# Value products of a gated feed-forward layer: one unit of two banks with 64-row parts in two row tiles, and a new order

## The chip, the cores and the metric

The kernel runs on one core of one Trainium2 chip. The metric is the device time of one execution in microseconds (us); the kernel before has a median of 239.88 us over 3 runs (239.53 to 241.89). All data are fp32 at the interface.

## The reference, cut to what matters

First a gated linear recurrence (mLSTM) over 768 steps, for 4 batches and 8 heads of 40 columns; then, over its 320 output columns, a causal convolution of 5 taps that gates a linear layer, and a second linear layer:

```python
# x: (4, 768, 320), the recurrence's output, heads side by side
xp = np.concatenate([np.zeros((B, K - 1, D)), x], axis=1)
for k in range(K):
    gate_pre += conv_w[k][None, None, :] * xp[:, k:k + S, :]
gate = 1.0 / (1.0 + np.exp(-gate_pre))
val = x @ w_val                      # the "value products"
return gate * val @ w_out            # the "output products"
```

The weights have 320 x 320 entries.

## The kernel before

**Tiling.** The 768 steps are cut into six chunks j of 128 steps (P), each of two halves of 64 (L). The recurrence is done in its chunked form: for each chunk, batch and half there are decays (`args` on PE, `expo` on ACT), scores (`scores` on PE, `probs` on DVE), weighted keys (`keyw` on POOL), products with the values and the state (`heads` on PE, fp32), and the copy of the new state (`state` on ACT). q and k are split into fp16 parts first (`hi` on POOL or ACT, `lo` on DVE, line 387) and turned, in chunk 0 and for q of chunk 1 by PE (`turn`, `tout`), later by transposing DMAs on SP's queue (`tr`). Then `rs` (POOL) and `x` (`gate_o`, DVE, line 496) give the recurrence's output, and `x_tr` (PE) and `xc` (ACT) turn it so that its 320 columns lie on partitions: 128 and 128 in `xc`, and the last 64 in `x3`, where batches 0 and 1 lie on partitions 0 to 63 and batches 2 and 3 on 64 to 127.

**The layer behind it**, `feed_part`, works on a chunk of all four batches (chunk 5 in two halves of two batches): `conv0` (ACT) and `conv` (DVE), the sigmoid `sig` (ACT), then for each block m of 128, 128 and 64 output columns a value product `val` (PE) and the product with the gate `z` (`z_mul`, DVE, line 591), then the output products `outp` (PE, lines 599 and 601) for two batches at a time, `ob` (ACT) and the store `od` (SP).

**A value product before.** For m = 0 and 1 it has one PSUM bank of 128 partitions x 512 (four batches of 128 steps). Two products over 128 rows each take all four batches at once (line 577). The last 64 rows of the contraction lie on two halves of the partitions, so two products over 128 rows of 256 columns (line 579) take `wv3[:, i]`, a copy of the 64 weight rows in half i with zeros in the other half; the zeros are set by `fill_v` (line 814). For m = 2 (64 columns) there are six products of 256 columns that write the two halves of the partitions (line 586). In the two halves of chunk 5 (line 574) the 64 rows are taken alone, without the zeros. The output products of a pair of batches already take their last 64 rows from two halves, into two banks (line 601).

**The order.** Nothing is reordered by a scheduler: `op` collects the work, and `PLAN` gives each kind's instances a place in one list of 1146; each engine, and each DMA queue, runs its own part of that list in order. `BANKS` gives the bank of each use of PSUM. Gates of the recurrence are computed by `gates` (DVE; 0 to 11 for the first 128 steps, 12 to 22 for the rest, interleaved by `PLAN`), spread to DRAM by `spr` (DMAs issued by ACT) and gathered by `gat` (SP); `args` of chunk 0 needs them. The weights are converted by `w_v` (DVE), `w_p` (POOL) and `w_a` (ACT).

Of the kernel before, what the change touches and what calls it, by code (L numbers as in the profile page):

```python
# [31 lines left out]
    "max": (  # L32
        "30 33 46 58 65 70 75 79 86 160 230 237 241 244 258 268 280 285 304 307 310 313 328 336 361 392 436 465 "
        "468 471 475 485 614 617 627 633 636 649 655 661 663 667 679 706 759 761 771 781"
    ),
# [6 lines left out]
    ),  # L42
    "lo": (
        "110 88 107 117 153 141 158 150 308 323 303 326 312 327 298 362 425 441 404 480 398 422 432 460 545 567 "
        "570 632 517 533 550 621 680 705 748 772 697 677 714 833 823 850 849 858 836 857 870 878"
    ),
# [3 lines left out]
    "args": (  # L50
        "176 187 182 191 223 231 219 260 263 272 291 348 365 376 396 410 433 476 488 523 551 580 540 588 597 642 "
        "637 648 698 718 707 774 788 785 817 839 873 889 893 909 918 974 953 1004 1016 1032 1030 1050"
    ),
    "expo": (
        "200 203 190 210 228 247 224 265 274 278 325 358 381 399 403 439 447 482 494 528 556 582 544 592 607 644 "
        "659 683 701 743 713 779 795 791 822 842 876 897 899 913 925 979 956 1009 1019 1042 1040 1055"
    ),
    "scores": (
        "197 199 194 222 234 236 250 275 345 347 370 367 380 394 446 461 478 481 492 558 564 591 576 594 640 646 "
        "669 699 744 747 741 784 819 837 851 872 883 901 910 921 971 980 996 1011 1053 1052 1054 1067"  # L60
    ),
    "probs": (
        "209 213 201 240 245 259 277 318 352 357 374 377 387 414 452 466 483 505 508 562 572 599 586 605 647 657 "
        "673 702 753 758 751 787 827 844 855 874 886 904 919 926 983 987 1002 1018 1056 1059 1058 1070"
    ),
    "keyw": (
        "205 212 202 225 232 257 251 270 286 311 332 372 391 405 411 449 472 486 499 553 569 593 573 601 631 650 "
        "662 691 709 755 717 783 799 797 825 852 881 900 916 922 929 960 1021 1043"
    ),
    "heads": (  # L70
        "214 226 207 243 254 266 283 322 356 371 386 400 428 448 463 484 547 559 534 568 583 625 619 629 685 700 "
        "690 710 762 778 768 794 847 866 861 885 895 914 940 955 998 1013 1007 1026 1060 1069 1065 1073"
    ),
    "state": (
        "221 235 215 253 262 273 299 333 366 457 397 417 444 462 479 490 552 574 541 579 598 653 626 643 692 712 "
        "703 754 769 786 775 802 862 880 868 890 902 920 948 970 1006 1012 1066 1068"
    ),
    "nabs": (
        "249 252 294 334 395 412 493 491 565 575 639 645 719 722 793 801 879 891 961 964 1024 1031 1072 1077"
    ),  # L80
    "nrec": "264 335 429 496 581 652 724 804 894 965 1033 1081",
    "rs": (
        "276 305 355 342 431 437 510 518 585 589 665 658 728 730 807 810 911 906 967 966 1036 1035 1083 1086"
    ),
    "x": (
        "282 320 393 354 473 458 520 526 603 595 684 660 731 734 814 846 917 912 973 969 1039 1037 1087 1088"
    ),
    "x_tr": (
        "287 338 408 363 495 521 527 530 671 616 715 721 792 835 905 903 968 959 982 984 1071 1048 1089 1092"
    ),  # L90
    "xc": (
        "293 343 413 369 500 525 532 535 675 620 735 739 812 838 915 907 977 972 986 988 1074 1051 1094 1098"
    ),
    "w_d": "89 63 43 98 93 87 229 220 302 382",
    "w_v": (
        "128 146 168 177 184 192 186 188 193 195 204 216 218 227 233 242 255 269 267 271 289 329 344 368 390 401 "
        "407 419 427 438 430 442 445 454 531 557"
    ),
# [6 lines left out]
    ),  # L105
    "conv0": "515 459 506 610 681 606 757 805 766 928 930 934 994 990 992 1078 1075 1080 1109 1103 1107",
    "conv": (
# [4 lines left out]
    ),  # L112
# [7 lines left out]
    ),  # L120
    "od": (
        "634 704 727 720 773 888 843 831 892 933 944 947 1001 1003 1028 1047 1063 1064 1095 1104 1137 1140 1143 "
        "1145"
    ),
}
# [19 lines left out]
def tile_mlstm_gated_ffn(  # L145
# [13 lines left out]
    nc = tc.nc  # L159
# [703 lines left out]
```

## Time and profile before

| what | us |
|---|---|
| median of 3 runs | 239.88 |
| the profiled execution | 239.03 |
| its span, first to last instruction | 237.2 |
| PE busy | 186.5 |
| DVE busy | 189.7 |
| ACT busy | 170.0 |
| POOL busy | 118.1 |

A row of the timeline reads: start in us from the span's start, duration in us, engine, line, operation, what is written from what, shape, count, and in brackets the idle time of the engine before it with what ended it. PE is the matmul engine, PEld its weight loads, SP the queue that issues most DMAs. An fp32 product is recorded as two matmuls. The end of a matmul is modelled and lies after the start of the next, so the pace of a series is read from starts.

### The profile page before, as it was taken

The page shows a single profiled execution, that of the slowest core. Times are in us where ns is not written, and L with a number is a line of the kernel's source. Part 1 is how long each engine was busy: PE and PEld are TensorE (multiplying, and loading weights), DVE is VectorE, ACT ScalarE, POOL GpSimd, SP SyncE. Part 2 cuts the span into 40 slices and gives each one's busy share as a digit, 9 for nine tenths or more (in the row PEclk, how much of TensorE's full clock was granted, in tenths as well). Part 3 has the DMA queues.
Part 4 walks back from the last instruction along what each step waited for, and adds up shares of the span by engine and source line. Part 5 has one row for each costly group of instructions (what it writes and reads, how often), then busy time and mean ns, then how long its engine had stood idle before and what let it go on. Part 6 is the DMA issues. An engine that isn't in the chain of part 4 may idle for free.

```text
span 237.2 us, 6282 instructions
## 1 busy us (share of the span) xinstructions
PE 186.5 (79%) x2392; PEld 131.8 (56%) x2392; DVE 189.7 (80%) x409; ACT 170.0 (72%) x353; POOL 118.1 (50%) x169
## 2 busy tenths in 40 slices
PE   0003266975877589869999899999999999999993
PEld 0003263854865365556757476676766765785541
DVE  6999989789998699999989398984796874449910
ACT  6716559699989999689989898787838737247411
POOL 8969734689795566376472737822813013001000
PEclk9999999798599979999999999999999999999998
DMA  7999359999799999999999999999950101011011
GB/s 134 172 181 190 40 99 152 194 150 196 154 165 183 185 169 161 191 170 171 174 199 173 217 186 199 205 172 144 168 148 0 58 6 53 0 59 55 3 55 57
DMA packets 146599, 31.96 MB, mean 135 GB/s; under 512 B 142408, under 2 KB 145864, under 8 KB 146568
## 3 DMA queue, kind: packets, MB, share of 16 engines
q1 hardware_dynamic: 144936, 31.25, 81.4%
q10 hardware_dynamic: 1632, 0.30, 0.7%
q8 instruction: 19, 0.31, 0.6%
q14 instruction: 12, 0.10, 0.1%
HBM read 17.87 MB, written 4.23 MB: 93 GB/s over the span
## 4 chain that ended last, share of the span: by engine, by line
PE 49%; DVE 21%; ACT 12%; POOL 5%; issue 5%; DMA 5%; SPq 0%; POOLq 0%; ACTq 0%; DVEq 0%
PE pb L599 11%; PE pb L463 10%; PE pb L577 5%; PE pb L574 4%; PE pb L601 4%; DVE stk L387 3%; PE pb L503 3%; DMA tq<-stk 3%; PE pb L434 3%; PE pb L579 3%; POOL stk L383 2%; PE pb L586 2%; DVE pb L545 2%; PE pb L421 2%; ACT junk L353 2%
## 5 line engine op out<-in xcount | busy, mean ns | idle before, releaser
L463 PE MATMUL pb<-vc,pt 104*64 104x41 f32 (+1 forms) x768 | 56.5, 237 | 7.8 <-DVE pt L439 3.6
L463 PEld LDWEIGHTS pb<-vc,pt 104*64 104x64 f32 (+1 forms) x768 | 51.2, 145 | 16.9 <-ACT vc L249 5.6
L446 POOL TENSOR_TENSOR kw<-kp,dm 128x320 f32<-128x320 f32 (+1 forms) x44 | 34.1, 782 | 51.2 <-ACT dm L424 27.0
L465 PE MATMUL pb<-vc,kw 128*40 128x41 f32 (+1 forms) x704 | 44.6, 220 | 1.7 <-ACT dm L424 0.7
L439 DVE SCALAR_TENSOR_TENSOR pt<-pb,cmp,dm 128x512 f32<-128x512 f32 x48 | 35.0, 742 | 11.2 <-PE pb L434 6.4
L465 PEld LDWEIGHTS pb<-vc,kw 128*40 128x40 f32 (+1 forms) x704 | 40.0, 120 | 2.3 <-issue 0.8
L410 PE MATMUL pb<-ident,stk 128*120 128x128 f16 x96 | 12.2, 313 | 30.5 <-DVE stk L387 30.4
L387 DVE SCALAR_TENSOR_TENSOR stk<-nat,scl,stk 128x320 f16<-128x320 f32 x48 | 32.6, 701 | 0.7 <-POOL stk L383 0.6
L424 ACT ACTIVATE dm<-pb 128x512 f32<-128x512 f32 x48 | 27.6, 594 | 4.5 <-PE pb L421 4.1
L383 POOL TENSOR_SCALAR stk<-nat,scl 128x640 f16<-128x640 f32 x28 | 25.2, 906 | 9.4 <-DVE scl L359 4.1
L599 PE MATMUL pb<-wall,zt 128*128 128x320 f32 x96 | 29.2, 444 | 0.0
L410 PEld LDWEIGHTS <-stk 128*120 128x120 f16 x96 | 10.7, 213 | 31.9 <-DVE stk L387 31.8
L545 DVE SCALAR_TENSOR_TENSOR pb<-xc,cwt,pb 128x512 f32<-128x512 f32 (+1 forms) x42 | 27.3, 671 | 1.4 <-ACT pb L541 1.0
L491 POOL TENSOR_TENSOR rs<-sg,den 128x320 f32<-128x320 f32 x24 | 18.1, 770 | 19.5 <-DVE den L487 15.6
L353 ACT ACTIVATE junk<-nat 128x320 bf16<-128x320 f32 x48 | 22.5, 468 | 6.0 <-DMA nat<-in_q_dram 3.4
L249 ACT COPY vc<-pb 40x328 f32<-40x328 f32 x44 | 18.9, 432 | 9.4 <-PE pb L465 7.6
L249 POOL COPY kp<-nat 64x640 f32<-64x640 f32 x24 | 22.5, 944 | 1.3
L249 ACT COPY ob<-pb 128x320 f32<-128x320 f32 x24 | 9.6, 426 | 17.3 <-PE pb L601 13.6
L434 PEld LDWEIGHTS <-tk 120*128 120x128 f16 x384 | 15.5, 100 | 11.1 <-issue 8.3
L434 PE MATMUL pb<-tq,tk 120*128 120x64 f16 x384 | 18.0, 196 | 4.5 <-ACT dm L424 2.6
L599 PEld LDWEIGHTS pb<-wall,zt 128*128 128x128 f32 x96 | 17.3, 190 | 7.6 <-issue 1.3
L577 PE MATMUL pb<-xc,wall 128*128 128x512 f32 x40 | 19.4, 607 | 0.5 <-ACT xc L249 0.5
(107 smaller groups left out, 350.0 us busy)
## 6 DMA issues: line engine op xcount, KB each, us to landing
sg<-in_o_gate_dram SPq DMA_DIRECT2D x6, 640.0 KB
vc<-in_v_dram SPq DMA_DIRECT2D x12, 320.0 KB
out_dram<-ob SPq DMA_DIRECT2D x24, 160.0 KB
nat<-in_q_dram SPq DMA_DIRECT2D x10, 320.0 KB
nat<-in_k_dram SPq DMA_DIRECT2D x10, 320.0 KB
nat<-in_q_dram SPq DMA_DIRECT2D x4, 160.0 KB
nat<-in_k_dram SPq DMA_DIRECT2D x4, 160.0 KB
raw<-in_moe_w_val_dram SPq DMA_DIRECT2D x2, 320.0 KB
```

The costliest lines, as they stand in the source:

```text
L249: (e.copy if e is nc.scalar else e.tensor_copy)(out, in_)
L383: nc.gpsimd.tensor_scalar(o, v, f, 1.0, op0=ALU.mult, op1=ALU.mult)
L387: nc.vector.scalar_tensor_tensor(t[:, :, lo : lo + D], part(j, x, i), scl[j % 2][:, x, i : i + 1], t[:, :, 0:D], op0=ALU.mult, op1=ALU.sub ...
L424: nc.scalar.activation(dm_[g % NDM], psd[g], AF.Exp)
L434: nc.tensor.matmul(pss[g][:, h], tk[h], tq[:, h], start=True, stop=True)
L439: nc.vector.scalar_tensor_tensor(pt_[g % NPT], pss[g], cmp_[j % 2][:, p, b : b + 1], dm_[g % NDM], op0=ALU.mult, op1=ALU.mult)
L446: eng("keyw", "P").tensor_mul(kw_[g % NKW][0:n], kp[0:n, p, b * H : (b + 1) * H], dm_[g % NDM][0:n, :, L - 1 : L].to_broadcast([n, H, D]),)
L463: nc.tensor.matmul(ph[u][p * L : (p + 1) * L, h], pt_[g % NPT][0:n, h], mv, start=True, stop=True)
L465: nc.tensor.matmul(pc[g][n0 : n0 + D, h], kw_[g % NKW][0:n, h], mv, start=True, stop=True)
L545: nc.vector.scalar_tensor_tensor(of(gt, c, b0, b1) if t == 4 else o, x, w, o, op0=ALU.mult, op1=ALU.add)
L577: nc.tensor.matmul(pf, wv[:, c, ms], x[:, c, :, 4:], start=(c == 0), stop=False)
L599: nc.tensor.matmul(t, zz[0][:, c, b], wo[:, c], start=(c == 0), stop=False)
```

## The change

For chunks 0 to 4, the value products of m = 0 and m = 1 (the weight columns, that is output rows 0 to 255 of the turned result) become one unit. It has two banks, one for each pair of batches, and each bank holds both blocks m side by side. Eight products of 256 columns take the first 256 rows; then four products of 64 rows take the last rows of each pair from its own half of the partitions, without zeros. `z_mul` now reads one bank, that is both blocks of one pair of batches. m = 2 and chunk 5 are computed as before. The zeros of `wv3` are only set for the 64 columns of m = 2. `PLAN` and `BANKS` are new throughout, with 1141 places; of their lines those that are spoken of are shown.

```diff
--- before.py
+++ after.py
@@ -16,123 +16,123 @@
...
 PLAN = {
-    "ld_g": "3 0",
-    "ld_q0": "13 21 26 32 35 24 28 47",
...
-    "gates": "27 42 34 37 55 62 66 77 91 95 103 105 29 49 44 57 68 84 99 119 123 129 134",
...
+    "ld_g": "35 32",
+    "ld_q0": "15 0 26 39 6 17 75 56",
...
+    "gates": "59 137 80 105 120 141 156 167 168 169 171 173 83 109 138 117 124 150 174 176 178 180 182",
...
-    "w_d": "89 63 43 98 93 87 229 220 302 382",
...
+    "w_d": "71 64 61 23 67 97 234 243 302 423",
...
-    "val": "415 507 498 674 725 733 821 853 840 962 946 975 1038 1044 1034 1096 1123 1112 1129 1118 1105",
-    "z": "578 590 584 736 740 746 863 867 865 978 976 981 1045 1049 1041 1127 1130 1122 1134 1132 1131",
-    "outp": "600 654 749 800 875 924 985 1017 1057 1076 1133 1135 1138 1141",
...
+    "val": "562 505 713 689 853 820 947 964 1014 1026 1090 1104 1099 1117 1122 1111",
+    "z": "588 583 580 729 731 727 872 870 862 969 967 973 1028 1031 1032 1123 1121 1120 1127 1129 1128",
+    "outp": "599 652 742 789 883 925 978 1002 1038 1071 1126 1130 1133 1136",
...
 BANKS = {
...
-    "val": "073310251234640712230",
-    "outp": "311751541632526116626547",
...
+    "val": "270507314471263371406",
+    "outp": "403206323674017663512173",
...
@@ -562,33 +562,44 @@
 
     vt, pot = {}, {}
 
-    def val(n, j, m, b0, b1):
+    def val(n, j, ms, b0, b1):
         x, y = xc[j % 2], x3[j % 2]
-        ms = slice(m * P, min(DM, m * P + P))
-        pf = vt[j, m, b0] = bank("val", n, b1 - b0 if m < 2 else B2, P)
+        cs = [slice(m * P, min(DM, m * P + P)) for m in ms]
+        ts = [bank("val", n + i, 2 * B2 if ms[0] < 2 and b1 - b0 == B else B2, P) for i in range(len(ms))]
+        vt[j, ms[0], b0] = ts
         if b1 - b0 < B:
             r = half(b0)
-            o = pf if m < 2 else pf[r]
-            mm = [(wv[:, c, ms], x[:, c, b0:b1, 4:]) for c in range(2)] + [(wv3[r, b0 // B2, ms], y[r, :, 4:])]
+            o = ts[0] if ms[0] < 2 else ts[0][r]
+            mm = [(wv[:, c, cs[0]], x[:, c, b0:b1, 4:]) for c in range(2)] + [(wv3[r, b0 // B2, cs[0]], y[r, :, 4:])]
             for i, (w, s) in enumerate(mm):
                 nc.tensor.matmul(o, w, s, start=(i == 0), stop=(i == len(mm) - 1))
-        elif m < 2:
-            for c in range(2):
-                nc.tensor.matmul(pf, wv[:, c, ms], x[:, c, :, 4:], start=(c == 0), stop=False)
-            for i in range(2):
-                nc.tensor.matmul(
-                    pf[:, i * B2 : (i + 1) * B2], wv3[:, i, ms], y[:, :, 4:], start=False, stop=(i == 1)
-                )
+        elif len(ms) == 2:
+            for m in range(2):
+                for c in range(2):
+                    for i, t in enumerate(ts):
+                        o = t[:, m * B2 : (m + 1) * B2]
+                        nc.tensor.matmul(
+                            o, wv[:, c, cs[m]], x[:, c, i * B2 : (i + 1) * B2, 4:], start=(m == 0 and c == 0), stop=False
+                        )
+            for m in range(2):
+                for i, t in enumerate(ts):
+                    r = half(i * B2)
+                    o = t[:, m * B2 : (m + 1) * B2]
+                    nc.tensor.matmul(o, wv3[r, i, cs[m]], y[r, :, 4:], start=False, stop=(m == 1))
         else:
             for c in range(3):
                 for i in range(2):
-                    w, s = (wv[:, c, ms], x[:, c, i * B2 : (i + 1) * B2, 4:]) if c < 2 else (wv3[:, i, ms], y[:, :, 4:])
-                    nc.tensor.matmul(pf[i * L : i * L + L], w, s, start=(c == 0), stop=(c == 2))
-
-    def z_mul(j, m, b0, b1):
-        s = vt[j, m, b0]
-        s = s[half(b0)] if m == 2 and b1 - b0 < B else s
-        nc.vector.tensor_mul(of(zz, m, b0, b1), s, of(gt, m, b0, b1))
+                    w, s = (wv[:, c], x[:, c, i * B2 : (i + 1) * B2, 4:]) if c < 2 else (wv3[:, i], y[:, :, 4:])
+                    nc.tensor.matmul(ts[0][i * L : i * L + L], w[:, cs[0]], s, start=(c == 0), stop=(c == 2))
+
+    def z_mul(j, m, i, b0, b1):
+        s = vt[j, m, b0][i]
+        if b1 - b0 == B and m == 0:
+            bs = slice(i * B2, (i + 1) * B2)
+            nc.vector.tensor_mul(zz[0][:, :, bs], s.rearrange("p (m b) t -> p m b t", m=2), gt[0][:, :, bs])
+        else:
+            s = s[half(b0)] if m == 2 and b1 - b0 < B else s
+            nc.vector.tensor_mul(of(zz, m, b0, b1), s, of(gt, m, b0, b1))
 
     def outp(j, bs):
         n = j * B + (2 * bs[0] if len(bs) > 1 else bs[0])
@@ -728,9 +739,10 @@
             for t in range(5):
                 op("conv" if t else "conv0", conv, n, j, c, t, b0, b1)
         op("sig", sigmoid, j, b0, b1)
-        for m in range(3):
-            op("val", val, seen.get("val", -1) + 1, j, m, b0, b1)
-            op("z", z_mul, j, m, b0, b1)
+        for ms in ((0, 1), (2,)) if b1 - b0 == B else ((0,), (1,), (2,)):
+            op("val", val, 3 * j + ms[0] + 3 * (b0 // B2), j, ms, b0, b1)
+            for i in range(len(ms)):
+                op("z", z_mul, j, ms[0], i, b0, b1)
         for bs in [(b, b + B2) for b in range(B2)] if b1 - b0 == B else [(b,) for b in range(b0, b1)]:
             op("outp", outp, j, bs)
             for b in bs:
@@ -811,7 +823,7 @@
             for t, r0 in ((wv3, 0), (wo3, L)):
                 for i in range(2):
                     if t is wv3:
-                        op("w_p", fill_v, "w_p", "P", t[L - i * L : P - i * L, i], 0.0)
+                        op("w_p", fill_v, "w_p", "P", t[L - i * L : P - i * L, i, 2 * P :], 0.0)
                     op("w_a", copy, "w_a", "A", t[i * L : i * L + L, i], w3[r0 : r0 + L])
             for c in range(2):
                 weights(wo[:, c], [w_out[c * P : (c + 1) * P]], 3 + c)
```

In the new list the unit of a chunk stands before its m = 2 product in chunks 3 and 4 and after it in chunks 0 to 2.

## Rows read from the trace of the kernel before

**Rows 1.** The page, part 1: busy us, share of the span, instructions.
```profile
PE 186.5 (79%) x2392; PEld 131.8 (56%) x2392; DVE 189.7 (80%) x409; ACT 170.0 (72%) x353; POOL 118.1 (50%) x169
```

**Rows 2.** Windows: stretch, length; busy (count) of PE, PEld, DVE, ACT, POOL; clock, DMA.
```profile
0.00:41.00 41.00, 11.12 (x101) 8.75 (x102) 36.80 (x96) 24.17 (x41) 28.98 (x49) 1.00 0.86 139
41.00:89.00 48.00, 36.46 (x664) 29.75 (x661) 42.40 (x86) 43.09 (x102) 34.91 (x44) 0.86 1.07 174
89.00:136.00 47.00, 41.64 (x605) 28.96 (x605) 41.52 (x89) 40.80 (x89) 26.87 (x36) 1.00 1.27 181
136.00:233.60 97.60, 97.26 (x1031) 64.31 (x1029) 68.95 (x143) 61.53 (x124) 27.34 (x42) 1.00 0.51 95
```

**Rows 3.** The chain of waits, its end: start us, us, what.
```profile
232.77 0.75 PE pb L601 x2
...
233.59 0.43 ACT ob L249
```

**Rows 4.** Timeline of PE, 134 to 139.5 us.
```profile
134.58 1.08 PE L586 MATMUL pb<-xc,wall 128*64 128x256 f32 x8 [1.05 <-DVE x L496]
...
136.74 2.40 PE L599 MATMUL pb<-wall,zt 128*128 128x320 f32 x8
```

**Rows 5.** The chain of waits, 120 to 146 us.
```profile
124.62 6.52 DMA tq<-stk
```

**Rows 6.** Timeline of DVE, 133.5 to 136.8 us.
```profile
134.03 0.49 DVE L496 TENSOR_TENSOR x<-pb,rs 128x320 f32<-128x320 f32 x1 [3.41 <-POOL rs L491]
...
135.18 1.62 DVE L591 TENSOR_TENSOR zt<-pb,sg 128x512 f32<-128x512 f32 x3
```

**Rows 7.** Timeline of PE, 195.8 to 202.7 us: value products of chunk 4.
```profile
197.31 1.98 PE L577 MATMUL pb<-xc,wall 128*128 128x512 f32 x4
199.13 1.03 PE L579 MATMUL pb<-x,wall 128*128 128x256 f32 x4
199.99 1.88 PE L577 MATMUL pb<-xc,wall 128*128 128x512 f32 x4
201.71 1.03 PE L579 MATMUL pb<-x,wall 128*128 128x256 f32 x4
202.57 0.38 PE L503 MATMUL pb<-ident,x 128*128 128x128 f32 x2
```

**Rows 8.** Timeline of PE, 191.3 to 194.3 us: output products of two batches.
```profile
193.53 0.81 PE L601 MATMUL pb<-wall,zt 64*128 64x320 f32 x4
194.27 0.25 PE L463 MATMUL pb<-vc,pt 104*64 104x41 f32 x1
```

**Rows 9.** Timeline of PE, 220.3 to 223.8 us: value products of chunk 5.
```profile
220.35 1.13 PE L574 MATMUL pb<-xc,wall 128*128 128x256 f32 x4
221.41 0.70 PE L574 MATMUL pb<-x,wall 64*128 64x256 f32 x2
222.04 1.13 PE L574 MATMUL pb<-xc,wall 128*128 128x256 f32 x4
```

**Rows 10.** Groups by shape: busy us, mean ns | idle before, releaser.
```profile
L387 DVE SCALAR_TENSOR_TENSOR stk<-nat,scl,stk 128x320 f16<-128x320 f32 x48 | 32.6, 701 | 0.7 <-POOL stk L383 0.6
...
L591 DVE TENSOR_TENSOR zt<-pb,sg 128x512 f32<-128x512 f32 x10 | 6.7, 686 | 3.6 <-PE pb L579 3.6
```

**Rows 11.** Timeline of SP's queue, 0 to 22 us.
```profile
1.20 0.41 SPq L832 DMA_DIRECT2D sg<-in_f_gate_dram  x1
1.65 0.43 SPq L336 DMA_DIRECT2D nat<-in_q_dram  x1
...
8.68 0.58 SPq L336 DMA_DIRECT2D nat<-in_q_dram  x1
```

**Rows 12.** Timelines of DVE, 0 to 42 us: first scan, last gate step, `probs`.
```profile
3.58 0.41 DVE L293 TENSOR_TENSOR_SCAN zt<-sg,ig 32x128 f32<-32x128 f32 x1 [1.30 <-DMA sg<-in_f_gate_dram]
...
21.32 0.69 DVE L305 TENSOR_TENSOR gsp<-ob,gsp 64x128 bf16<-64x128 f32 x1
...
40.99 0.74 DVE L439 SCALAR_TENSOR_TENSOR pt<-pb,cmp,dm 128x512 f32<-128x512 f32 x1
```

More of the change, by code (lines that the diff above doesn't have):

```diff
@@ L56 @@
-        "659 683 701 743 713 779 795 791 822 842 876 897 899 913 925 979 956 1009 1019 1042 1040 1055"
+        "229 247 244 240 277 288 272 293 316 327 340 361 358 378 392 403 417 502 515 491 591 578 596 614 641 647 "
+        "670 679 695 744 716 749 767 821 777 818 838 897 877 915 926 980 907 982 1036 1027 1039 1059"
     ),
     "scores": (
-        "197 199 194 222 234 236 250 275 345 347 370 367 380 394 446 461 478 481 492 558 564 591 576 594 640 646 "
-        "669 699 744 747 741 784 819 837 851 872 883 901 910 921 971 980 996 1011 1053 1052 1054 1067"
+        "241 226 246 258 284 289 291 307 324 332 359 356 396 384 401 419 485 495 501 531 584 587 594 634 642 677 "
@@ L61 @@
+        "681 686 708 760 753 758 807 817 812 831 880 909 878 914 972 992 945 994 1033 1046 1048 1062"
     ),
     "probs": (
-        "209 213 201 240 245 259 277 318 352 357 374 377 387 414 452 466 483 505 508 562 572 599 586 605 647 657 "
-        "673 702 753 758 751 787 827 844 855 874 886 904 919 926 983 987 1002 1018 1056 1059 1058 1070"
+        "245 254 249 264 295 298 303 310 337 341 363 373 400 440 413 426 490 506 520 535 597 592 601 637 649 685 "
+        "690 693 715 769 756 764 813 830 822 837 884 911 890 920 981 997 962 1017 1040 1049 1054 1065"
@@ L72 @@
-        "690 710 762 778 768 794 847 866 861 885 895 914 940 955 998 1013 1007 1026 1060 1069 1065 1073"
+        "250 267 260 275 300 317 326 338 344 362 375 391 406 451 422 439 526 537 543 557 615 628 621 645 668 696 "
+        "702 728 732 775 765 782 828 840 845 869 904 918 896 938 988 1009 998 1030 1050 1064 1060 1066"
     ),
     "state": (
-        "221 235 215 253 262 273 299 333 366 457 397 417 444 462 479 490 552 574 541 579 598 653 626 643 692 712 "
-        "703 754 769 786 775 802 862 880 868 890 902 920 948 970 1006 1012 1066 1068"
+        "263 280 270 283 312 323 333 352 355 438 386 399 415 465 436 482 533 546 554 564 624 636 630 654 684 703 "
@@ L77 @@
+        "710 733 739 803 774 800 832 871 859 874 913 928 902 946 999 1004 1056 1063"
     ),
     "nabs": (
-        "249 252 294 334 395 412 493 491 565 575 639 645 719 722 793 801 879 891 961 964 1024 1031 1072 1077"
+        "278 287 335 346 370 427 489 497 567 563 643 653 705 735 784 793 863 881 959 957 1023 1034 1067 1069"
     ),
-    "nrec": "264 335 429 496 581 652 724 804 894 965 1033 1081",
+    "nrec": "290 347 437 500 568 656 736 794 882 960 1037 1070",
     "rs": (
-        "276 305 355 342 431 437 510 518 585 589 665 658 728 730 807 810 911 906 967 966 1036 1035 1083 1086"
+        "299 304 357 365 446 442 504 509 573 571 660 662 747 746 802 799 885 888 963 965 1044 1043 1073 1075"
@@ L84 @@
     ),
     "x": (
-        "282 320 393 354 473 458 520 526 603 595 684 660 731 734 814 846 917 912 973 969 1039 1037 1087 1088"
+        "308 360 367 377 460 448 512 514 579 575 663 671 773 748 847 849 891 917 977 979 1057 1045 1079 1080"
     ),
     "x_tr": (
-        "287 338 408 363 495 521 527 530 671 616 715 721 792 835 905 903 968 959 982 984 1071 1048 1089 1092"
+        "313 372 388 382 468 463 522 534 595 589 755 683 810 836 875 912 968 970 983 985 1068 1058 1083 1086"
     ),
     "xc": (
-        "293 343 413 369 500 525 532 535 675 620 735 739 812 838 915 907 977 972 986 988 1074 1051 1094 1098"
+        "348 380 394 389 484 470 528 539 605 600 761 687 815 841 887 919 971 975 989 991 1072 1061 1091 1095"
@@ L93 @@
     ),
[L94 removed]
+    "w_d": "71 64 61 23 67 97 234 243 302 423",
     "w_v": (
[L96 to L98 removed]
[3 rows of a table removed]
+        "88 113 140 142 149 170 154 186 192 204 224 227 233 235 238 239 259 268 271 279 315 321 379 393 407 416 "
+        "434 445 464 473 467 471 477 479 494 503"
+    ),
[3 rows of a table added]
     "tr": (
[2 rows of a table removed]
[2 rows of a table added]
     ),
[L106 removed]
+    "conv0": "450 447 519 612 609 603 805 780 770 930 936 922 995 1001 1018 1074 1081 1076 1097 1109 1107",
@@ L107 @@
     "conv": (
[4 rows of a table removed]
-    ),
[4 rows of a table removed]
[4 rows of a table added]
+    ),
[4 rows of a table added]
     "ob": (
[2 rows of a table removed]
[2 rows of a table added]
     ),
     "od": (
-        "634 704 727 720 773 888 843 831 892 933 944 947 1001 1003 1028 1047 1063 1064 1095 1104 1137 1140 1143 "
-        "1145"
+        "620 743 707 709 762 850 848 844 898 903 944 942 987 990 1015 1013 1052 1053 1088 1092 1132 1135 1138 "
+        "1140"
     ),
@@ L126 @@
 BANKS = {
-    "turn": "201374652700",
-    "args": "013456165235714473316523713617154535223300255357",
-    "scores": "562421362335334446426665740463237430556467135033",
-    "ph": "074165124125022674107247",
-    "pc": "23352155227733552542007447647733036065443010205",
-    "x_tr": "261154424465732057130204",
-    "conv": "675650004756046513564",
-    "val": "073310251234640712230",
-    "outp": "311751541632526116626547",
+    "turn": "035214670217",
+    "args": "456253054116722220154136320117150322715637044021",
+    "scores": "432504700614456444555014006335324055110067647044",
+    "ph": "623501366516421627255123",
+    "pc": "44375644173345241133224470663034305631416020700",
+    "x_tr": "766401332772034403237672",
+    "conv": "724753757036037640552",
+    "val": "270507314471263371406",
+    "outp": "403206323674017663512173",
 }
```

18 lines of the change are left out of this document (8 added, 10 removed), and 60 rows, old and new, of the table PLAN.

## The prediction

> **What bounds the kernel now.** I read the page first, for the share of each engine: no engine is busy for more than 80% of the span, DVE 189.7 us and PE 186.5 us [rows 1]. Such shares are means over stages, so I cut the span where the picture changes. Up to 136 us PE works for 11.12 + 36.46 + 41.64 = 89.2 us and is idle for 46.8; from 136 to 233.6 us it works for 97.26 us of 97.60 [rows 2]. In that second part nothing but PE sets the pace: the chain of waits ends in output products on PE, back to back, and one copy [rows 3]. So the end of PE is its work plus its idle time ahead: 186.5 + 47.1 = 233.6 us. A change moves the end by what it takes out of PE's work, and by what it adds to or takes from those 47 us.
>
> What makes the 47 us is mostly DVE: it is busy 36.80 of the first 41.00 us, 42.40 of the next 48.00 and 41.52 of the next 47.00 [rows 2]. It is the bound up to about 120 us, with ACT close behind it from 41 to 89 us (43.09 of 48.00). The last idle of PE before it fills up comes at 134.58 us, where a value product waits 1.05 us for its bank, whose last reader is `gate_o` (L496) on DVE; PE is at the first output products of chunk 1 at 136.74 us [rows 4], right behind the z products of DVE at 135.18 us [rows 6]. That x and these z products hang on a transposing DMA of 6.52 us, which held a slot of `stk` [rows 5].
>
> **The unit, step by step.** An fp32 product is two passes in the records (eight records of L577 for the four instructions of chunk 4 [rows 7]). Four passes of 512 columns run from 197.31 to 199.13 us, the first of them after another shape; in the next product they run from 199.99 to 201.71, 1.72 us, 0.43 each. Four passes of 256 columns take 199.13 to 199.99, 0.86 us, 0.215 each [rows 7]. One product of 128 rows is thus 1.72 + 0.86 = 2.58 us, or 2.68 where it begins after another shape; both together 5.26 as in chunk 4, or 5.36 where other work stands between them, as in chunks 0 to 3 of before.
>
> The new unit has the same columns for the first two thirds of the contraction, cut in 256s: 2 m x 2 c x 2 banks x 2 passes = 16 passes x 0.215 = 3.44 us (eight passes of 512 cost 8 x 0.43 = 3.44 too). For the last 64 rows before spends 8 passes of 256 columns, half of whose weights are zeros: 1.72 us. The new unit gives each pair of batches only its own 64 rows. Do two such passes run side by side? L601 is the nearest row: four records of 320 columns with 64 rows, two halves into two banks, take 193.53 to 194.27, 0.74 us; one after the other they would take 4 x 0.267 = 1.07, in pairs 2 x 0.267 = 0.53 and two changes of shape. So they pair [rows 8]. The change of shape I price at L574: four full passes and the step to 64 rows are 220.35 to 221.41, 1.06 us = 4 x 0.215 + 0.20, that is 0.10 at the entry and 0.10 at the step; the two 64-row passes 221.41 to 222.04, 0.63 = 2 x 0.215 + 0.20 [rows 9]. For the new unit: 0.10 entry + 3.44 + 0.10 + four paired passes 0.86 + 0.20 = 4.70 us. Against 5.30 (mean of 5.26 and 5.36) a unit saves 0.60, or 0.70 where no change of shape stands at its start; five units, 3.0 to 3.5 us, say 3.2. Bounds: if each second batch of 64-row passes did not pair, 8 x 0.215 stands for 4 x 0.215 and the unit is 5.56, 1.0 to 1.5 us lost over five; if no change of shape cost anything, 4.30 and 5 us gained. I take the paired value, for L601 has the same row halves and the same two banks.
>
> A rule that speaks against the change: the Trainium skill, TensorEngine Tiling (Array Packing), Key Properties, says that changing the tiling mode, not just the tile, drains the engine. If that meant waiting until the last full pass is out, whose record lasts 0.38 us (1.03 less three steps of 0.215) [rows 7], a step would cost 0.17 instead of 0.10 us. Two steps in each of five units would then make the saving 0.7 us smaller, 2.5 us. The trace has the step at 0.10, so I stay with that.
>
> **What else the change moves.** The z products stay ten of 512 elements, 686 ns each [rows 10], each now reading one bank with both blocks of rows instead of one block with all batches. They wait for the whole unit instead of one product; the output products needed all of them anyway, so that costs nothing as long as the order puts other PE work between (4 to 8 PE steps do in the new list). The two memsets of zeros shrink from 320 to 64 columns on POOL, in a stretch where POOL has room: nothing.
>
> **The new order** is the larger unknown. At the start it asks for the gates as the 7th and 8th load instead of the 1st and 2nd. Before, the second of them goes out at 1.20 us and the first scan runs at 3.58; q and k loads go out at 1.65 to 8.68 us [rows 11, 12]. Eight issues at 0.5 to 0.8 us put the gates' landing near 8 us, and the last half of chunk 0's q (now the 16th) near 14 to 17. The new order gives DVE 6.6 us of constants ahead of the scan, so only 1 to 2 us of that is idle; later DVE stands at the scales of the last batch and at the first tap conversion, some 2 to 5 us. The gates are ready near 34 us instead of 21.32 + 0.69 [rows 12], and the first `probs` of batch 0 come near 50 instead of 40.99 us. This is mostly work drawn forward: summed over the lists with the records' durations, DVE has 36.3 us ahead of those `probs` in the old order (its busy time to 41 us, 96 instructions, is 36.80 [rows 2]) and 45.3 in the new one, seven `lo` steps of chunk 1 (701 ns each [rows 10]) and five weight conversions being most of the difference. Ahead of the first `probs` of chunk 2 both orders have the same, 79.0 and 79.3 us (79.2 is DVE's busy time up to 89 us [rows 2]); the sigmoid of chunk 0 has 2.5 us more ACT work ahead, that of chunk 1 0.5 us less. So by chunk 2 the new kernel is level if DVE loses no more than the 10 us it loses now up to 89 us. Against it stand 2 to 4 us more of idling at the start; for it, that there is less room for small waits later, and that the z products of chunk 1 no longer stand behind an x of chunk 3, where DVE now idles 3.41 us behind that DMA [rows 5, 6]. I take these as equal: PE's idle time stays 47 us, give or take 4.
>
> **Sum.** 3.2 us off 239.03 us (span 237.2 and 1.8 around it) is 235.8 us for the profiled execution. The median of the runs shown is 239.88, 0.85 more, so 236.7 us.
>
> **Rivals.** (1) The start costs more than it gives: the late gates and the q load behind the taps hold DVE for more than 6 us over before, and the work drawn forward doesn't pay that back by 136 us. From 3.2 us of extra PE idle the gain is gone; 6 to 9 us give 242.5 to 246. For it: DVE has little idle to catch up with [rows 2]. Against: the equal sums at chunk 2. Chance 0.13. (2) The front runs ahead: the DMA wait [rows 5] goes and PE fills up 2 to 4 us earlier: 231.5 to 234.5 us. Chance 0.17. (3) The front is 2 to 3 us late and eats most of the saving: 238 to 241 us. Chance 0.17. (4) The 64-row passes don't pair: 5.56 us a unit, 240 to 241.5. L601 speaks against it. Chance 0.05. (5) The unit waits for banks: it needs two free at once where a product needed one, and waits such as the 1.05 us at 134.58 [rows 4] come once a unit, 3 us in all: 239 to 240. In the Trainium skill the same page, Gotcha 1: PSUM Pressure, says that row tiles must write to different banks and so raise the pressure on PSUM; the two banks of the unit are that. Against it: from 136 us on PE has 0.3 us of idle in all [rows 2], so the old banks come free early, and the new list leaves 5 or more steps between release and unit in most chunks. Chance 0.06.
>
> **Numbers.** The forecast, 234.8 to 238 us, has 0.42. A measurement of this kernel can tell about 1% (2.4 us) from no change. Faster by over 1% (under 237.5): 0.37 of the forecast and rival 2, 0.54. Slower by over 1% (over 242.3): rival 1 and a little of 3 and 4, 0.17. The rest, 0.29, is within 1%. The range 231.5 to 242 leaves out most of rival 1 and the far side of rival 2.
>
> **What would show it.** The unit: from its first pass to the next product 4.6 to 4.7 us, 64-row records starting in pairs; 5.5 us means rival 4. PE idle up to its full stretch near 47 us, and nothing after; a wait before the first pass of a unit, ended by a reader of its bank, is rival 5. First `probs` near 50 us and those of chunk 2 at 87 to 92; later than 94 us is rival 1. What would make me wrong most easily is a load or DMA at the start that lands later than its bytes suggest, since DVE works strictly in order and everything of chunk 0 is behind it.

## The result, and the profile after

The changed kernel takes 237.11 us (median of 4 runs, 236.31 to 237.54), the kernel before 239.99 on the same chip (4 runs): ratio 0.988, 95% interval 0.9836 to 0.9924. That is 1.2% faster, 2.9 us. The forecast was 236.7 us. Here and below, medians are over all runs of a kernel, while ratios, and the differences in us worked out from them, leave out the few runs that fell into a slower state of the chip.

The profiled execution took 236.31 us, with a span of 234.5. Its page, part 1, answers to [rows 1]:

```profile
PE 183.6 (78%) x2432; PEld 135.4 (58%) x2432; DVE 190.0 (81%) x409; ACT 169.4 (72%) x353; POOL 113.4 (48%) x169
```

PE has 2.9 us less work; the other engines but POOL are where they were. The windows, with the columns of [rows 2]:

```profile
0.00:41.00 41.00, 7.44 (x64) 6.63 (x64) 38.03 (x98) 22.91 (x47) 25.49 (x47) 0.84 0.99 153
41.00:89.00 48.00, 37.85 (x718) 30.61 (x719) 41.55 (x84) 46.32 (x104) 32.78 (x43) 0.85 1.12 170
89.00:136.00 47.00, 44.31 (x641) 33.47 (x641) 42.84 (x90) 40.05 (x80) 28.13 (x39) 0.93 1.20 181
136.00:231.00 95.00, 93.95 (x1011) 64.67 (x1009) 67.60 (x139) 59.68 (x125) 27.05 (x42) 1.00 0.54 93
```

Until 136 us PE works for 89.60 us, before for 89.22: it starts later and makes it up. It ends at 230.90 us, so its idle time is 230.90 - 183.55 = 47.3 us, before 47.0. Work fell by 2.9, idle rose by 0.3, the end came 2.6 us earlier. The end is still output products (now L610 and L612) back to back, in the chain of waits, as [rows 3]:

```profile
228.89 1.27 PE pb L610 x4
230.16 0.75 PE pb L612 x2
230.98 0.42 ACT ob L249
```

The unit of chunk 3 in PE's timeline, to be held against [rows 7], and the z products of chunk 1 with the first output product behind them, against [rows 4, 6]:

```profile
134.59 0.70 PE L610 MATMUL pb<-wall,zt 128*128 128x320 f32 x2
...
173.51 3.70 PE L581 MATMUL pb<-xc,wall 128*128 128x256 f32 x16
177.14 1.14 PE L588 MATMUL pb<-x,wall 64*128 64x256 f32 x8
178.21 1.08 PE L593 MATMUL pb<-xc,wall 128*64 128x256 f32 x8
```

```profile
132.21 0.42 DVE L602 TENSOR_TENSOR zt<-pb,sg 128x256 f32<-128x256 f32 x1 [0.89 <-ACT sg L558]
132.55 1.28 DVE L599 TENSOR_TENSOR zt<-pb,sg 128x512 f32<-128x512 f32 x2
```

The unit takes 173.51 to 178.21, 4.70 us. Sixteen passes take 3.63 us to the first 64-row record, then eight records of 64 rows 1.07: four pairs of 0.216, which is 0.86, and 0.21 for the change of shape in and behind them. The groups by shape (busy us, mean ns, then idle before) show that no unit waited for a bank in this execution, and that z products cost what they cost before:

```profile
L581 PE MATMUL pb<-xc,wall 128*128 128x256 f32 x80 | 18.5, 384 | 0.0
L588 PE MATMUL pb<-x,wall 64*128 64x256 f32 x40 | 5.7, 402 | 0.0
```

```profile
L599 DVE TENSOR_TENSOR zt<-pb,sg 128x512 f32<-128x512 f32 x10 | 6.4, 682 | 1.4 <-ACT sg L558 1.3
```

### The profile page after: what moved, and what is told of

Same layout as the page of the kernel before. It is cut to its first block, busy times and chain, and to the rows that moved or that the text cites. A ratio compares the mean times of both kernels' runs of the same rounds, so it can differ in the third digit from the quotient of the medians.

```text
span 234.5 us, 6368 instructions
## 1 busy us (share of the span) xinstructions
PE 183.6 (78%) x2432; PEld 135.4 (58%) x2432; DVE 190.0 (81%) x409; ACT 169.4 (72%) x353; POOL 113.4 (48%) x169
## 4 chain that ended last, share of the span: by engine, by line
PE 41%; ACT 17%; DVE 13%; DMA 12%; SPq 8%; issue 5%; POOL 1%; ACTq 1%; POOLq 0%; DVEq 0%
PE pb L463 12%; PE pb L610 9%; DVE pb L545 5%; DMA tk<-stk 5%; PE pb L581 5%; SPq L336 5%; PE pb L612 3%; DMA sg<-in_o_gate_dram 3%; ACT junk L353 3%; PE pb L421 3%; PE pb L434 3%; DMA nat<-in_q_dram 2%; ACT sg L558 2%; SPq L844 2%; PE pb L503 2%
## 5 line engine op out<-in xcount | busy, mean ns | idle before, releaser
L463 PE MATMUL pb<-vc,pt 128*64 128x41 f32 (+1 forms) x768 | 54.5, 236 | 6.2 <-ACT vc L249 4.8
L463 PEld LDWEIGHTS pb<-vc,pt 128*64 128x64 f32 (+1 forms) x768 | 49.9, 143 | 13.7 <-ACT vc L249 6.2
L465 PE MATMUL pb<-vc,kw 128*40 128x41 f32 (+1 forms) x704 | 44.1, 218 | 0.6 <-ACT x L249 0.2
L439 DVE SCALAR_TENSOR_TENSOR pt<-pb,cmp,dm 128x512 f32<-128x512 f32 x48 | 34.4, 736 | 11.0 <-PE pb L434 8.6
L383 POOL TENSOR_SCALAR stk<-nat,scl 128x640 f16<-128x640 f32 x28 | 26.0, 938 | 21.4 <-DMA vc<-in_v_dram 10.3
L387 DVE SCALAR_TENSOR_TENSOR stk<-nat,scl,stk 128x320 f16<-128x320 f32 x48 | 32.1, 688 | 4.9 <-POOL stk L383 2.5
L545 DVE SCALAR_TENSOR_TENSOR pb<-xc,cwt,pb 128x512 f32<-128x512 f32 (+1 forms) x42 | 27.4, 673 | 3.6 <-ACT pb L541 3.1
L610 PE MATMUL pb<-wall,zt 128*128 128x320 f32 x96 | 29.1, 442 | 0.1
L381 ACT ACTIVATE stk<-nat,scl 128x640 f16<-128x640 f32 x20 | 16.0, 823 | 9.9 <-DMA gda<-gsp 5.3
L610 PEld LDWEIGHTS pb<-wall,zt 128*128 128x128 f32 x96 | 17.3, 190 | 7.8 <-issue 1.3
L434 PE MATMUL pb<-tq,tk 120*128 120x64 f16 x384 | 18.6, 196 | 4.0 <-ACT vc L249 2.3
L421 PE MATMUL pb<-ra,la 120*128 120x512 bf16 x48 | 18.1, 404 | 1.1 <-DVE sg L545 0.9
```

The source lines that it names most:

```text
L383: nc.gpsimd.tensor_scalar(o, v, f, 1.0, op0=ALU.mult, op1=ALU.mult)
L387: nc.vector.scalar_tensor_tensor(t[:, :, lo : lo + D], part(j, x, i), scl[j % 2][:, x, i : i + 1], t[:, :, 0:D], op0=ALU.mult, op1=ALU.sub ...
L434: nc.tensor.matmul(pss[g][:, h], tk[h], tq[:, h], start=True, stop=True)
L439: nc.vector.scalar_tensor_tensor(pt_[g % NPT], pss[g], cmp_[j % 2][:, p, b : b + 1], dm_[g % NDM], op0=ALU.mult, op1=ALU.mult)
L463: nc.tensor.matmul(ph[u][p * L : (p + 1) * L, h], pt_[g % NPT][0:n, h], mv, start=True, stop=True)
L465: nc.tensor.matmul(pc[g][n0 : n0 + D, h], kw_[g % NKW][0:n, h], mv, start=True, stop=True)
```

## The experiments: unit and order apart

My theory: the end is PE's work and a front that VectorE and ScalarE set; the unit saves 3.3 us of work in any order, and the new order by itself is neutral. First rival: the new order made the gain.

**The new order without the unit.** In `val`, the loops of the unit give way to the two old products; `z_mul` takes one block again, and the fill of zeros is that of before (cut at the three dots):

```
-            for m in range(2):
+            for m, t in enumerate(ts):
                 for c in range(2):
-                    for i, t in enumerate(ts):
...
+                    nc.tensor.matmul(t, wv[:, c, cs[m]], x[:, c, :, 4:], start=(c == 0), stop=False)
+                for i in range(2):
+                    nc.tensor.matmul(
+                        t[:, i * B2 : (i + 1) * B2], wv3[:, i, cs[m]], y[:, :, 4:], start=False, stop=(i == 1)
+                    )
...
+            nc.vector.tensor_mul(of(zz, i, b0, b1), s, of(gt, i, b0, b1))
```

> The order of work and the banks of the changed kernel, but the two products of 128 output rows of chunks 0 to 4 done as before: one batch range of 512 columns after the other, the 64-row parts over 128 rows filled up with zeros, and one bank for each product. Theory (the unit's shorter work is the whole gain): two products take 5.3 to 5.4 us where the unit takes 4.7, so five times 0.67 us come back, 237.1 + 3.3 = 240.4 us, 239.6 to 241.2, and PE's busy time is 186.5 to 187. Rival (the new order made the gain): 237.1 to 238 us. Rival (the new order costs, and the unit brought more than the difference of the two kernels shows): above 241.2 us.

Measured: 238.58 us, ratio to the kernel before 0.9963 (0.9923 to 1.0002). The changed kernel, run again later beside the kernel before:

> The changed kernel itself, for the comparisons with the other runs on one chip. If its gain over the kernel before is 2.9 us as first measured: 237.1 us; if part of that was the chip: 237.5 to 238.2 us.

It took 237.26 us, ratio 0.9888 (0.9844 to 0.9932). So the new order alone is worth 0.9 us, between nothing and 1.8, and the unit in it some 1.9 (0.9963 less 0.9884, the mean of the two ratios, of 239.7 us), give or take 1.4, where I had 3.3. The profiled executions show where the rest may have gone. PE's work differs by 3.0 us (186.54 and 183.55), its end by 2.2 (233.10 and 230.90), its idle time by 0.8 the other way. PE's timeline around 146 us, with the old products in the new order:

```profile
145.87 0.81 PE L606 MATMUL pb<-wall,zt 64*128 64x320 f32 x4
146.61 0.41 PE L434 MATMUL pb<-tq,tk 120*128 120x64 f16 x8
...
148.00 0.39 PE L434 MATMUL pb<-tq,tk 120*128 120x64 f16 x8
```

and in the changed kernel, in the first of its two profiled executions (236.31 us):

```profile
144.68 0.81 PE L612 MATMUL pb<-wall,zt 64*128 64x320 f32 x4
145.90 0.39 PE L434 MATMUL pb<-tq,tk 120*128 120x64 f16 x8 [0.41 <-ACT vc L249]
...
147.91 0.39 PE L434 MATMUL pb<-tq,tk 120*128 120x64 f16 x8
```

and in the second, of the run above (238.10 us):

```profile
146.08 0.81 PE L612 MATMUL pb<-wall,zt 64*128 64x320 f32 x4
146.82 0.41 PE L434 MATMUL pb<-tq,tk 120*128 120x64 f16 x8
...
148.21 0.39 PE L434 MATMUL pb<-tq,tk 120*128 120x64 f16 x8
```

In the first, PE is 1.19 us ahead of the old products at these output products and 0.09 ahead at 148 us: it waited for ScalarE's copies. Of the 1.19, though, 0.47 were there ahead of the first unit. In the second, PE is 0.21 us behind at both places: it loses nothing here, but it waits 0.49 and 0.97 us at 159 and 162 us. The same kernel thus ends at 230.90 us in one execution and at 232.68 in the other, 2.2 and 0.4 us ahead of the one execution with the old products. What holds in both, and in the profiled executions of the two later runs that keep these units (other pass order, gates first), is this: the unit of chunk 3 saves 0.64 us and that of chunk 4 0.55, and PE loses nothing behind them. What the units of chunks 0, 1 and 2 save, 0.1 to 0.65 us each at once, is kept or waited away, another way in each execution.

**The unit without row tiles.** The 64-row parts go over 128 rows, half zeros, and the fill of zeros is that of before:

```
-                    nc.tensor.matmul(o, wv3[r, i, cs[m]], y[r, :, 4:], start=False, stop=(m == 1))
+                    nc.tensor.matmul(o, wv3[:, i, cs[m]], y[:, :, 4:], start=False, stop=(m == 1))
```

> The changed kernel, with the same unit of two banks and the same order of its full products, but the 64-row parts over all 128 rows of a zero-filled weight, so that no two passes lie in different row tiles. Theory (the row tiles make the gain): eight passes of 216 ns in place of four pairs, without the two changes of shape, 24 x 216 + 83 = 5.27 us for the unit against 4.69, so five times 0.58: 237.1 + 2.9 = 240.0 us, 239.2 to 240.8. Rival (the two banks and the alternation of the full passes make the gain): unit near 4.7 us, 237.1 us, 236.5 to 237.8.

Measured: 239.32 us, ratio 0.9989 (0.995 to 1.0027). The unit of chunk 3 in its timeline of PE:

```profile
176.53 3.70 PE L581 MATMUL pb<-xc,wall 128*128 128x256 f32 x16
180.07 1.89 PE L587 MATMUL pb<-x,wall 128*128 128x256 f32 x8
181.89 1.08 PE L592 MATMUL pb<-xc,wall 128*64 128x256 f32 x8
```

5.36 us against 4.70, and 5.26 to 5.36 for the two old products: the two banks give nothing, the row tiles all of the unit's saving.

**The 64-row passes in another order.**

```
-            for m in range(2):
-                for i, t in enumerate(ts):
+            for i, t in enumerate(ts):
+                for m in range(2):
```

> The changed kernel, with the 64-row passes of a unit in another order: the two products of one pair of batches (one row tile) first, then the two of the other, so that only the middle pass has a neighbour in the other row tile. Theory (a pass runs beside its neighbour only, so the alternation of the row tiles makes the pairs): the four records of one tile follow each other at 216 ns, then the other four, the unit takes 4.7 + 3 x 0.216 = 5.3 to 5.5 us, and the time is 237.1 + 3 to 4 = 240 to 241 us. Rival (the engine takes a later pass of the other tile ahead, or 64-row passes overlap whatever their order): unit 4.7 us, 236.5 to 237.8 us.

Measured: 237.81 us, ratio 0.9914 (0.9877 to 0.9952). My theory fell. The unit of chunk 3:

```profile
175.28 3.70 PE L581 MATMUL pb<-xc,wall 128*128 128x256 f32 x16
178.91 1.14 PE L588 MATMUL pb<-x,wall 64*128 64x256 f32 x8
179.98 0.87 PE L593 MATMUL pb<-xc,wall 128*64 128x256 f32 x6
```

4.70 us again: eight records in 1.07 us are four pairs, though the program has four passes of one row tile ahead of the four of the other. The records do not name the row tile. But two 64-row passes of a single row tile, in the kernel before, follow one another: 0.63 us [rows 9], where a pair would take 0.42. So the passes of the second row tile run beside those of the first, without alternating in the program.

This run also bears on what a unit is worth. Over the three measurements with units of 4.7 us (0.988, 0.9888, 0.9914) and the two with 5.3 us in the same order (0.9963, 0.9989) the means differ by 0.0082, or 2.0 us, give or take 0.9.

**The unit in the old order.** The code of the unit with the order and banks of before, each unit at the later place of its two products (chunk 0: slot 507 in place of 415 and 507). Against the plan of the kernel before:

```
-    "val": "415 507 498 674 725 733 821 853 840 962 946 975 1038 1044 1034 ...",
+    "val": "507 498 725 733 853 840 962 975 1044 1034 ...",
```

> The unit of the changed kernel in the order and the banks of the kernel before; the unit stands where the later of its two products stood. Theory (the unit's shorter work is the whole gain, and the idle time at the front is the same in both orders): 240.0 - 3.3 = 236.7 us, 236.2 to 237.5. Rival (the new order made the gain, or is needed for it: the unit's first product waits longer, its z products crowd): 239 to 240.5 us, with new waits of PE beside the units.

Measured: 241.88 us, ratio 1.009 (1.0052 to 1.0128): 2.2 us slower than before, not 3.3 faster. Nor did the rival foresee a loss of this size. My next theory was the late place: the first product of chunk 0 stood in a stretch where PE idles. One run moves that product alone, in the kernel before:

```
-    "val": "415 507 498 ...",
+    "val": "506 507 498 ...",
```

> The kernel before, with nothing changed but the place of one product: the product of output rows 0 to 127 of chunk 0 goes from slot 415, where PE otherwise idles near 77 us, to slot 506, beside the second product. Theory (the unit in the old order lost by this place: 2.7 us of work leave the idle stretch, PE idles 5 us there and then runs at half the clock for some us): 242 to 245 us against 239.7, with 5 us of idle time near 77 us and slow passes behind it. Rival (the place is nothing, since the front is set by VectorE and ScalarE, and the unit itself is what costs in the old order): 239.5 to 240.5 us.

Measured: 240.17 us, ratio 1.0038 (1.0012 to 1.0064), 0.9 us (0.3 to 1.5): it may be a part of the 2.2, but not the whole. Another puts the units of chunks 1 to 4 early and leaves chunk 0 alone (again against the plan of before):

```
+    "val": "415 507 498 688 733 829 853 957 975 1038 1034 ...",
...
-    "val": "073310251234640712230",
+    "val": "073310215234640712230",
```

> The order of the kernel before, with the unit in chunks 1 to 4 at the place of the earlier of its two products, or as close to it as two banks are free (slots 688, 829, 957 and 1038), and chunk 0 with the two old products at their old places (no two banks are free there early). Theory (the unit saves its shorter work in any order, and the unit in the old order lost by its late places: the first product of chunk 0 no longer ran in the 5 us in which PE idles near 77 us): four times 0.67 us less than the kernel before, 239.7 - 2.7 = 237.0 us, 236.4 to 238.2, and PE's idle time near 47 us again. Rival (the unit does not go with the old order at all, by its banks or its z products): 239.5 to 242 us, with waits of PE at the units.

In it I had overlooked two argument products of chunk 3 (slots 698 and 707) in a bank of chunk 1's unit, so a part of that chunk's values is overwritten and the products wait on one another; its 245.18 us tell nothing of the question. With free banks:

```
-    "val": "415 507 498 688 733 ...",
+    "val": "415 507 498 702 733 ...",
-    "args": "013456165235714473316523713617154535223300255357",
+    "args": "013456165235714473316523713617654535223300255357",
```

> As the run before with units at early places in the old order, but with two banks that are free: the unit of chunk 1 at slot 702, and one argument product of chunk 3 in another bank. Chunk 0 keeps its two old products. Theory (the unit saves 0.67 us in each of four chunks in any order, as long as no product loses its cover): 239.7 - 2.7 = 237.0 us, 236.2 to 238.2. Rival (the old order does not go with units, whatever their place): 239.5 to 242 us.

Measured: 245.29 us, ratio 1.0234 (1.0187 to 1.0282), 5.6 us slower: this theory fell too. Its trace shows where. Up to 123 us PE runs the instructions of the kernel before in their order, 2.5 us later in this execution. The lag is 5.9 us behind the products of chunk 1, 7.9 behind those of chunk 2, 7.4 at the end. PE's timeline (in this kernel L587 and L594 are the unit, L599 the product of 64 output rows), then VectorE's:

```profile
125.34 0.31 PE L463 MATMUL pb<-vc,pt 128*64 128x41 f32 x2 [1.28 <-ACT junk L353]
...
127.13 0.25 PE L463 MATMUL pb<-vc,pt 128*64 128x41 f32 x1 [0.66 <-DVE x L496]
...
129.79 3.72 PE L587 MATMUL pb<-xc,wall 128*128 128x256 f32 x16
133.44 1.14 PE L594 MATMUL pb<-x,wall 64*128 64x256 f32 x8
...
138.95 1.69 PE L599 MATMUL pb<-xc,wall 128*64 128x256 f32 x8 [1.96 <-DVE x L496]
```

```profile
136.00 0.17 DVE L475 TENSOR_SCALAR den<-pb 128x8 int32<-128x8 int32 x1 [3.66 <-PE pb L463]
...
138.41 0.49 DVE L496 TENSOR_TENSOR x<-pb,rs 128x320 f32<-128x320 f32 x1 [1.18 <-POOL rs L491]
```

Three things add up. Where the first product filled a wait, PE now waits (1.28 and 0.66 us). The block of 4.7 us stands ahead of a step of heads (L463) for which VectorE waits 3.66 us and then, for POOL, another 1.18; then PE waits 1.96 us for VectorE. In the kernel before VectorE waited 3.41 us in this place, for POOL alone [rows 6], and PE 1.05 [rows 4], so 1.4 and 0.9 us of this are new. And behind that wait PE is slow, by 0.5 us (a lag of 5.4, then of 5.9); windows with the granted clock third from the end:

```profile
136.98:138.95 1.97, 0.01 (x2) 0.00 (x1) 0.73 (x2) 1.97 (x1) 1.97 (x3) 1.00 1.07 201
138.95:142.69 3.74, 3.74 (x36) 2.37 (x37) 2.85 (x6) 3.65 (x9) 2.91 (x7) 0.55 1.01 167
142.69:145.80 3.11, 3.11 (x18) 1.76 (x15) 3.08 (x5) 1.61 (x5) 0.48 (x1) 1.00 0.46 93
```

The last of these runs keeps the units to chunks 3 and 4:

```
+    "val": "415 507 498 674 725 733 821 853 840 957 975 1038 1034 ...",
```

> The kernel before with the unit in chunks 3 and 4 alone, at slots 957 and 1038, where PE is never idle; chunks 0 to 2 keep their two products and their places. Theory (the unit saves its shorter work where PE is full, and what the old order lost with units it lost in chunks 0 to 2, where VectorE and ScalarE set the pace and a block of 4.7 us in PE's queue makes them wait): 239.4 - 1.1 = 238.3 us, 237.5 to 239.0. Rival (a unit costs in the old order wherever it stands): 240 us and more.

Measured: 239.63 us, ratio 1.0008 (0.9972 to 1.0045): no loss, and not the 1.1 us either. In its trace the lag behind the kernel before is 1.09 us ahead of chunk 3's products and 1.09 behind them: the 0.55 us are lost again in the two places where the two products had stood, 0.30 in the first, with a wait of 0.22 us that they had covered, and 0.25 in the second, with one of 0.09. Chunk 4's unit gains 0.55. So in the old order the unit costs in chunks 1 and 2, where VectorE and ScalarE set the pace, and saves little behind. How the loss with late units (2.2 us) divides between the three was not taken apart further.

**The start.**

```
-    "ld_g": "35 32",
+    "ld_g": "-1 -2",
```

> The changed kernel with its two gate loads first in SP's queue, as near as the kernel before had them. Theory (the late start is made up before 60 us since VectorE and ScalarE fill the time with other work, so the start does not set the end): 0 to 1 us less than the changed kernel. Rival (the late first probs, 49.2 against 41.0 us, cost time that a start as before would give back): 2 to 4 us less.

Measured: 236.75 us, ratio 0.9877 (0.9833 to 0.9921) beside 0.9888 for the changed kernel: 0.3 us less, give or take 1.5: no difference that can be told. The late gates cost nothing that these runs show.

**The tail.** Six half products of the last chunk make way for one unit and one product of 64 output rows, both at slots behind the last xc; the z products stay per half:

```
-    "val": "... 1014 1026 1090 1104 1099 1117 1122 1111",
+    "val": "... 1014 1026 1096 1109",
-    "z": "... 1031 1032 1123 1121 1120 1127 1129 1128",
+    "z": "... 1031 1032 1115 1115 1127 1128",
```

> The changed kernel with the value products of the last chunk in one unit too (both pairs of batches, 4.7 us, the full passes of the first pair of batches ahead) and one product of 64 output rows (1.45 us), where the changed kernel takes six half products of 1.6 to 1.7 us (9.9 us); its z products per half of the batches. Theory that PE alone sets the end: 3.7 us less than the changed kernel. Theory that the front of the last chunk is set by VectorE and ScalarE (taps of the second half to 223.1 us, its sigmoid, its z products to 225.2 us, then two output products of 2.03 us): the end of PE goes from 230.9 to 229.3 us, 1.6 us less than the changed kernel, 1.0 to 2.0. Rival (the z products and the taps get into each other's way): no gain, or up to 1 us more.

Measured: 242.46 us, ratio 1.0073 (1.0032 to 1.0115), 1.7 us more than the kernel before and 4.4 us more than the changed kernel by the ratios. PE's timeline and windows (in this kernel L588 is the product of 64 output rows, L606 the output products):

```profile
219.22 0.60 PE L588 MATMUL pb<-x,wall 128*64 128x256 f32 x4
223.62 2.16 PE L606 MATMUL pb<-wall,zt 128*128 128x320 f32 x4 [3.80 <-DVE sg L545]
...
227.07 2.50 PE L606 MATMUL pb<-wall,zt 128*128 128x320 f32 x4
```

```profile
219.80:223.60 3.80, 0.02 (x2) 0.00 (x0) 3.58 (x9) 0.63 (x2) 0.00 (x0) 1.00 0.00 0
223.60:227.10 3.50, 3.48 (x7) 1.48 (x7) 1.59 (x3) 1.04 (x2) 0.00 (x0) 0.56 0.00 0
227.10:230.90 3.80, 3.80 (x8) 1.68 (x7) 0.00 (x0) 0.43 (x1) 0.00 (x0) 0.51 0.12 43
```

The z products were done by 221.5 us, but the first output product waited 3.80 us for a tap (L545): its bank was that of the second half's 64-row taps, whose last reader I had moved behind. The two output products then ran at half the clock, 3.5 and 3.8 us in place of 2.0. One digit puts it into bank 0:

```
-    "outp": "403206323674017663512173",
+    "outp": "403206323674017663510173",
```

> The last chunk's unit as before, and one thing more: the first output product of the last chunk takes a bank that nothing holds (bank 0), where it took the bank of the 64-row taps of the second half and so waited for their last one (PE idle for 3.8 us to 223.6 us, and the two output products behind it at half the clock, 3.6 us each). Theory (that bank was the whole loss): outputs begin at 220.6 to 221.6 us, PE ends near 229.3 us in the changed kernel's clock, 235.3 to 236.4 us, 1 to 2 us less than the changed kernel. Rival (PE waits for the taps by another way, or its idle time of 1 to 2 us between the products and the outputs lowers the clock again): 238 us and more.

Measured: 234.42 us, ratio 0.9774 (0.9734 to 0.9813), faster than both kernels; 2.7 us less than the changed kernel by the ratios (0.0114 of 239.7), give or take 1.4. PE's timeline:

```profile
217.86 0.60 PE L588 MATMUL pb<-x,wall 128*64 128x256 f32 x4
219.83 1.34 PE L606 MATMUL pb<-wall,zt 128*128 128x320 f32 x4 [1.37 <-DVE zt L594]
...
224.15 1.34 PE L606 MATMUL pb<-wall,zt 128*128 128x320 f32 x4 [0.23 <-DVE zt L594]
```

I had expected 1 to 2 us. In this execution the front is 0.5 us earlier, and the third output product starts on the first z product of its half, 0.4 us ahead of the end of the second. PE now waits for z: VectorE sets the end of the tail, with ScalarE's sigmoid (L552), for which that z product had waited 0.70 us.

## Why the prediction was right, and where not

**End = PE's work + its idle time: right.** The sum always holds; what was forecast is that work falls by 3.2 us and that idle time stays 47 us, nearly all of it ahead of 136 us. It is 183.55 + 47.3 = 230.9 us, with 0.9 us of idle time behind 136 us. In the second execution it is 183.7 + 49.0 = 232.7, with 1.7 us behind 136: the idle time moves by 1.7 us between executions of one kernel, which is more than half of the saving that is looked for.

**The unit: right to 0.01 us.** From its first pass to the next work the five units take 4.72, 4.61, 4.72, 4.69 and 4.72 us in the trace, mean 4.69; 4.70 was forecast. The 64-row passes pair (rival 4 is out). The way to 64 rows and back costs 0.30 us, as the sum had it: 0.09 ahead of the first of them (3.63 us to it, 3.54 where passes over 128 rows follow) and 1.07 - 4 x 0.216 = 0.21 in and behind the eight. That is 0.15 for each of the two changes. The Trainium skill, TensorEngine Tiling (Array Packing), Key Properties, has a change of mode drain the engine; read as the wait for a whole pass, 0.17 us each, that is 0.34 us in place of 0.30, and five units would save 0.2 us less, not 0.7. There the prediction compared wrongly: it set 0.10 for one change against that reading, while its own sum has 0.30 for the two, and 0.30 is too near 0.34 to speak against it. z products: 682 ns, as forecast; no waits for banks of the size of rival 5, which is out.

**The step that was mis-sized: five units x 0.64.** I let every unit count. The five are worth 1.9 us beside the old products in the new order (give or take 1.4), 2.0 over all five measurements in that order (give or take 0.9), not 3.2. The units of chunks 3 and 4 kept theirs, 0.64 and 0.55 us, in all four profiled executions. What the first three saved met waits of PE that differ from one execution to the next, so how much of it counts is shown by the medians alone, and which waits take it is not shown.

**The new order as equal: off by about as much the other way.** It gives 0.9 us (0 to 1.8) with the old products. The step named for it did happen: the z products of chunk 1 start at 132.21 us, not behind an x of chunk 3 at 135.18 [rows 6], and the output products behind them at 134.59 in place of 136.74 [rows 4]. With the old products in the new order these start at 135.78, and in the changed kernel's second execution at 135.99, so some 1 us of it is the order's, as far as single executions tell. Whether the 0.9 us come from this step was not tested. So the sum came out at 2.9 us for 3.2, from two terms that I had as 3.2 and 0: that the number is so near is luck. Rivals 2 and 3 were this term with either sign, and neither came near its size.

**The start: near what was said, and harmless.** In the trace of VectorE the first scan, the last gate step and the first `probs`:

```profile
10.27 0.79 DVE L293 TENSOR_TENSOR_SCAN zt<-sg,ig 32x128 f32<-32x128 f32 x1
...
33.27 0.28 DVE L305 TENSOR_TENSOR gsp<-ob,gsp 64x128 bf16<-64x128 f32 x1
...
49.23 1.41 DVE L439 SCALAR_TENSOR_TENSOR pt<-pb,cmp,dm 128x512 f32<-128x512 f32 x2 [0.34 <-ACT dm L424]
```

10.27 us for the 8 forecast, 33.27 for 34, 49.23 for 50; the idle time of 2 to 5 us at the scales and taps did not come (38.03 of the first 41 us are busy). The first `probs` of chunk 2 come at 88.37 us, before at 88.95: 8 us late had become level, as the equal sums of work said. Rival 1 is out, and the run with the gates first shows nothing that the start had to give, within 1.5 us.

**What I did not see at all:** that the unit depends on the order. I had treated the two as separate terms; in the old order, at the places that I tried, the kernel is 2.2 us slower with all five units late, 5.6 with four early, and no faster with the last two alone. Whether another place in the old order would pay was not tried.

## What to carry to other kernels

A saving on an engine counts for sure only where that engine no longer waits for another; what is saved ahead of such a wait can be waited away, so count the pieces behind the last wait in full and the others in part. Take two executions of one kernel before a difference between two traces is read as the change: here the same kernel ended 1.8 us apart. Two pieces merged into one lose the wait that one of them filled, and put a longer block ahead of what other engines wait for: price the merge in the order in which it will stand. When work is moved ahead, follow the last reader of every bank that it writes, and count a wait of TensorE of some us with the slow passes behind it.

## What the runs showed of the hardware

**The clock behind a wait.** In the changed kernel PE is idle from 77.2 to 80.8 us; then the granted clock is at its lower level, 1.2 GHz. It is at that level again in the stretch from 90.8 us; from 84.4 to 90.8 PE was idle for 2.3 us:

```profile
77.20:80.80 3.60, 0.00 (x0) 0.00 (x0) 3.56 (x12) 3.40 (x6) 1.44 (x2) 0.75 1.26 219
80.80:84.40 3.60, 3.60 (x65) 3.52 (x65) 2.05 (x5) 3.54 (x11) 2.33 (x5) 0.50 1.36 134
...
90.80:93.50 2.70, 2.70 (x12) 1.19 (x12) 2.67 (x7) 1.85 (x6) 2.21 (x3) 0.50 1.26 203
```

The product of 64 output rows of chunk 0 falls in the last of these stretches and takes 2.76 us, those of later chunks 1.35 to 1.45. The waits of 1.96 us (0.55 behind it) and of 3.80 us (0.56 and 0.51) shown above did the same; the wait of 1.37 us in the tail was followed by output products at full speed (1.34 us for four passes).

**Row tiles overtake.** 64-row passes issued as four of one row tile and then four of the other ran in pairs. That is read from their time, since the records do not name the row tile. The Trainium skill, TensorE: Matmul & The Clock Gate, Part 3, says that matmuls start and end strictly in order; the 1.07 us for eight such records do not fit that, and the measurement decides.
